# Windowed attention with sinks, then an RWKV channel mix: q kept in even/odd token order and read in steps by the score matmuls

## The chip, the cores and the metric

The kernel runs on one core of one Trainium2 chip. The metric is the device time of one launch in microseconds. All times given for a profile are of one profiled execution; the times of a kernel are those of runs without one.

## What is computed

```python
# q, k, v: (4, 8, 768, 64) = batch, heads, tokens, head size; n_sink = 4, window = 128
scores = (1 / sqrt(64)) * q @ k^T
keep = (key < 4) | ((query - key >= 0) & (query - key < 128))
a = softmax(where(keep, scores, -1e9))
x = (a @ v), heads joined                       # (4, 768, 512)

x_prev = x shifted by one token (zeros first)
xk = mu_k * x + (1 - mu_k) * x_prev             # xr likewise with mu_r
kk = relu(xk @ w_k) ** 2                        # 512 -> 1024
out = sigmoid(xr @ w_r) * (kk @ w_v)            # (4, 768, 512), float32
```

Inputs and output are float32; the kernel multiplies in bf16.

## The kernel before

The work is cut into 12 units of 256 tokens, three per batch entry (u = 3b + T, with T = 0, 1, 2). For each unit there are four stages in the code: `prepare` (casts and transposes of k and q, cast of v), `attend` (scores, exponential, mask, products with v, division), `mix` (transpose of x, the two mixtures xk and xr) and `ffn` (the three products with weights, relu and square, gate, output).

The order in which they run is not the order of the code. Every step is entered in a plan (`P.op`) with an engine, a cost, the data that it reads and writes, and the pool buffers that it takes or holds. The order on each engine is then a fixed list of step numbers (`ORDER`), and for some steps the engine is a fixed choice (`CHOICE`). The planner simulates that order with the costs to decide which buffer of a pool each step gets, and where it puts warm-up matmuls on TensorE (L1019) while TensorE would wait early on. So a step that is left out of the plan would renumber all behind it.

The path of q, which the change touches:

- *Load.* A unit of q is [8 heads, 256 tokens, 64] in float32. For units 0 to 7 (L413) a partition p gets the tokens 2p and 2p + 1 of each head, which lie side by side in memory, so that a row of the transfer has 512 bytes. For units 8 to 11 (`QD`, by `by_dma`) and for units 5 to 11 of k (`KD`) the two halves of 128 tokens are loaded one by one, with rows of 256 bytes (L406).
- *Cast* to bf16 into `qb` (L605, L602), on ScalarE, VectorE or GpSimd.
- *Transpose*, so that the head size lies on the partitions, two heads (a "head pair" c) in 128 partitions. Units 0 to 7: on TensorE through a PSUM bank (L631), one 128 x 128 matmul for the even and one for the odd tokens of each head pair; then a copy (L639) brings the bank to `qt` and, by reading the bank in steps, puts the tokens back into their natural order. Units 8 to 11: by a DMA transpose from `qb` to `qt` (L619), one for each half of 128 tokens, which are in natural order already.
- *Use.* `qt` has the layout [128, head pair, 2, 128]. The sink scores (L697, T > 0) have the keys of the four sinks as stationary operand and all 256 queries of `qt` moving. The window scores (L728) have 64 or 128 keys of one head as stationary operand, in one quarter or half of the array, and 64 to 256 queries moving. Two heads and two halves of the keys run side by side. They are issued two head pairs at a time into two PSUM tiles `sc` (24 matmuls for T > 0, 8 for T = 0). ScalarE then takes the exponential (L787), VectorE multiplies by the mask (L801), and TensorE multiplies by v (L820) and adds the sinks' part (L775).

k takes the same path, and is not changed.

SyncE issues nearly all DMAs, in the order of its list: loads, DMA transposes and outputs (L1015) stand in one queue.

Of the kernel before, what the change touches and what calls it, by code (L numbers as in the profile page):

```python
# [136 lines left out]
    ),  # L137
}

# [1 line left out]
class Plan:  # L141
# [17 lines left out]
    def op(self, engine, cost, emit, rank, reads=(), writes=(), take=(), hold=(), port=False,  # L159
           lag=None, service=0.0, descs=128, mode=0, alts=None, room=2080):  # L160
        i = len(self.ops)
        if i in CHOICE:
            engine = CHOICE[i]
            cost, emit, port = alts[engine]
        self.ops.append(dict(alts=alts,engine=engine, cost=cost, emit=emit, rank=rank, reads=list(reads),
                             writes=list(writes), take=list(take), hold=list(hold), port=port,
                             lag=(1300.0 if service else 90.0) if lag is None else lag,
                             service=service, descs=descs, mode=mode, room=room))

    def schedule(self):  # L170
        ops = self.ops
# [134 lines left out]
def kernel(  # L306
# [14 lines left out]
    nc = tc.nc  # L321
# [67 lines left out]
    def load(u, names, rank, h0=0, h1=H):  # L389
        b, T = divmod(u, NT)  # L390
        for name in names:
            key = (name, u)
            if name == "v":
                for g in range(2):
                    s0 = 256 * T + 128 * g
                    P.op("SP", 600.0, lambda key=key, g=g, s0=s0: nc.sync.dma_start(  # L396
                        out=buf[key][:, g, :, :],
                        in_=v[b, :, s0:s0 + 128, :].rearrange("h p d -> p h d")), rank,
                        service=1250.0, descs=1024, take=[] if g else [("vs", key)],
                        hold=[key] if g else [], writes=[(name, u, g)])  # L400
                continue
            src = {"k": k, "q": q}[name]
            if by_dma(name, u):
                for g in range(2):
                    s0 = 256 * T + 128 * g
                    P.op("SP", 600.0, lambda key=key, src=src, g=g, s0=s0: nc.sync.dma_start(  # L406
                        out=buf[key][:, 4 * g:4 * g + 4, :, :].rearrange("p h j d -> p (h j) d"),
                        in_=src[b, :, s0:s0 + 128, :].rearrange("h p d -> p h d")), rank,
                        service=1250.0, descs=1024, take=[] if g else [(name + "s", key)],
                        hold=[key] if g else [], writes=[(name, u, g)])  # L410
                continue

            P.op("SP", 530.0, lambda key=key, src=src: nc.sync.dma_start(  # L413
                out=buf[key][:, h0:h1, :, :].rearrange("p h j d -> p h (j d)"),
                in_=src[b, h0:h1, 256 * T:256 * T + 256, :].rearrange(
                    "h (p j) d -> p h (j d)", j=2)), rank,
                service=128 * (h1 - h0) * 1.82, descs=128 * (h1 - h0),
                take=[] if h0 else [(name + "s", key)], hold=[key] if h0 else [],
                writes=[(name, u, c) for c in range(h0 // 4, h1 // 4)])

    def load_weight(what, rank):
        name, part = what[:2], what[2:]
# [171 lines left out]
    def prepare(u, rank):  # L594
        b, T = divmod(u, NT)
        for name, half in (("k", 0), ("q", 0), ("k", 1), ("q", 1)):
            key, psk = (name + "t", u), ("prep", u, name, half)
            raw, rk = (name, u), (name + "b", u)
            hs = slice(4 * half, 4 * half + 4)
            def cast(copy, raw=raw, rk=rk, hs=hs, half=half, name=name):  # L600
                if by_dma(name, u):
                    return lambda: copy(  # L602
                        out=buf[rk][:, half, :, :].rearrange("p h d -> p (h d)"),
                        in_=buf[raw][:, hs, :, :].rearrange("p h j d -> p (h j d)"))
                return lambda: copy(  # L605
                    out=buf[rk][:, :, hs, :].rearrange("p j h d -> p h j d"),
                    in_=buf[raw][:, hs, :, :])

            P.op("ACT", act(512), cast(nc.scalar.copy), rank + half,
                 alts={"ACT": (act(512), cast(nc.scalar.copy), False),  # L610
                       "DVE": (dve(512, 0.52), cast(nc.vector.tensor_copy), True),
                       "POOL": (600.0, cast(nc.gpsimd.tensor_copy), True)},
                 take=[] if half else [(name + "b", rk)],
                 hold=[raw] + ([rk] if half else []),
                 reads=[(name, u, half), "table"],
                 writes=[rk + (half,)])

            if by_dma(name, u):
                P.op("SP", 1240.0, lambda key=key, rk=rk, half=half: nc.sync.dma_start_transpose(  # L619
                    out=buf[key][:, :, half, :],  # L620
                    in_=buf[rk][:, half, :, :].rearrange("p h d -> p (h d)")), rank + half,
                    service=930.0, descs=512, lag=1300.0, room=1200, reads=[rk + (half,)],
                    take=[] if half else [(name + "t", key)],
                    hold=[rk] + ([key] if half else []), writes=[key + (half,)])
                continue

            def transpose(half=half, psk=psk, rk=rk):
                ps = buf[psk].bitcast(BF16)[:, 0:512].rearrange("p (j t) -> p j t", j=4)
                for j in range(4):
                    c = 2 * half + j // 2  # L630
                    nc.tensor.transpose(  # L631
                        out=ps[:, j, :], identity=ident,
                        in_=buf[rk][:, j % 2, 2 * c:2 * c + 2, :].rearrange("p a d -> p (a d)"))

            P.op("PE", 225.0, transpose, rank + half, lag=PE_LAG, take=[("bank", psk)],
                 reads=["ident", rk + (half,)], writes=[psk], hold=[rk])

            def evacuate(copy, half=half, psk=psk, key=key):
                return lambda: copy(  # L639
                    out=buf[key][:, 2 * half:2 * half + 2, :, :].rearrange(  # L640
                        "p c g (t j) -> p c (g t) j", j=2),
                    in_=buf[psk].bitcast(BF16)[:, 0:512].rearrange(
                        "p (c j t) -> p c t j", c=2, j=2))

            P.op("ACT", 600.0, evacuate(nc.scalar.copy), rank + half,
                 alts={"ACT": (600.0, evacuate(nc.scalar.copy), False),
                       "DVE": (625.0, evacuate(nc.vector.tensor_copy), False)},
                 hold=[psk] + ([key] if half else []),
                 take=[] if half else [(name + "t", key)],
                 reads=[psk] + ([key + (0,)] if half else []), writes=[key + (half,)])  # L650
# [35 lines left out]
    def attend(u, rank):  # L686
        b, T = divmod(u, NT)
        both = b in JOINT
        if T == 1 or T == 2 and not both:
# [3 lines left out]
            def sink_scores():  # L693
                for i, w in enumerate(us):
                    for c in range(NP):
                        r0 = 32 * (c // 2) + 64 * (c % 2)
                        nc.tensor.matmul(out=buf[psk][r0:r0 + 32, 256 * i:256 * i + 256],  # L697
                                         lhsT=ksink[b % 2][:, 32 * c:32 * c + 32],
                                         rhs=buf["qt", w][:, c, :, :], start=True, stop=True)

            P.op("PE", 150.0 + 109.0 * (len(us) - 1), sink_scores, rank, lag=PE_LAG, mode=2,
                 take=[("bank", psk)], hold=[("qt", w) for w in us], writes=[psk],
# [9 lines left out]
        def scores(k):  # L712
            c = k
            kt, qt, sc = buf["kt", u], buf["qt", u], buf["sc", u, k]
            qs = qt[:, c, :, :].rearrange("p g t -> p (g t)")
            jobs = [(kt[:, c, 0, :], 128, 0, 256), (kt[:, c, 1, :], 384, 128, 256)]
            if T > 0:
                jobs.append((buf["kt", u - 1][:, c, 1, :], 0, 0, 128))
            for (lhs, o0, q0, q1) in jobs:
# [5 lines left out]
                for a in range(2):  # L725
                    rows = slice(64 * a, 64 * a + 64)
                    for keys, f0, f1 in parts:
                        nc.tensor.matmul(out=sc[keys, a, o0 + f0 - q0:o0 + f1 - q0],  # L728
                                         lhsT=lhs[rows, keys], rhs=qs[rows, f0:f1],
                                         start=u not in BIAS, stop=True,  # L730
                                         skip_group_check=u in BIAS)

# [342 lines left out]
```

## Time and profile before

| | |
|---|---|
| time, median of 3 runs | 170.36 us (169.63 to 170.5) |
| span of the profiled execution | 167.0 us (its time with start and end is not listed) |
| TensorE (PE) busy | 159.0 us, 95% of the span |
| VectorE (DVE) busy | 150.6 us, 90% |
| ScalarE (ACT) busy | 127.6 us, 76% |
| GpSimd (POOL) busy | 19.3 us, 12% |
| DMA packets | 80726, of them 61625 under 512 bytes; 33.85 MB |
| mean granted clock of TensorE | 0.990 |

How to read it: the span runs from the first to the last instruction. A row names the line of the kernel, engine, operation, destination and sources, tile of the array or shape, the count, busy time and the mean of one. PEld is TensorE's loading of the stationary operand, which overlaps with its matmuls; SPq is the queue of DMA issues of SyncE. A matmul's duration includes its way through the array, so matmuls overlap; what a group of them occupies is the time from its start to the start of what follows.

### The profile page before, as it was taken

The numbers are of one execution on the slowest core, as the hardware profiler recorded it, in microseconds if no ns is written. First come the engines' busy times: TensorE is split into PE (matmuls) and PEld (weight loads), VectorE is DVE, ScalarE is ACT, GpSimd is POOL, SyncE is SP. The second block draws the span as 40 slices with busy tenths as digits, with TensorE's granted clock in tenths as the row PEclk, the third lists the DMA queues.
The fourth block names the chain that finished last, engine by engine and source line by source line (L and its number), as shares of the span: only waits on it lengthen the run. The fifth ranks groups of instructions, "written<-read, shape, count | busy, mean of one in ns | idle before, by whom it ended". The sixth has DMA issues, their size and how long they took to land.

```text
span 167.0 us, 4741 instructions
## 1 busy us (share of the span) xinstructions
PE 159.0 (95%) x1870; PEld 103.0 (62%) x1870; DVE 150.6 (90%) x391; ACT 127.6 (76%) x210; POOL 19.3 (12%) x46
## 2 busy tenths in 40 slices
PE   7967999999999999999999999999999999999992
PEld 2436566845558666667557675765577575677551
DVE  7179999999999999989999999899999979998941
ACT  3497898998599999988998999889839729652120
POOL 5731020000343121220001000000000000000000
PEclk9996899999999999999999999999999999999999
DMA  4999989999989999889998997896899443410033
GB/s 139 242 291 354 330 219 383 364 216 292 259 219 277 150 266 227 191 206 276 232 182 150 243 265 103 215 211 148 191 203 268 88 92 112 188 67 0 0 135 116
DMA packets 80726, 33.85 MB, mean 203 GB/s; under 512 B 61625, under 2 KB 75201, under 8 KB 80705
## 3 DMA queue, kind: packets, MB, share of 16 engines
q1 hardware_dynamic: 80688, 33.56, 86.3%
q8 instruction: 14, 0.23, 0.6%
q14 instruction: 8, 0.06, 0.1%
q10 hardware_dynamic: 16, 0.00, 0.0%
HBM read 24.12 MB, written 6.29 MB: 182 GB/s over the span
## 4 chain that ended last, share of the span: by engine, by line
PE 78%; ACT 8%; SPq 6%; DMA 5%; issue 1%; DVE 1%
PE bank L950 21%; PE bank L999 21%; PE bank L981 11%; PE bank L820 6%; PE sc L728 5%; DMA ks<-in_k_dram 5%; ACT e L787 3%; PE bank L1019 3%; SPq L396 3%; PE bank L631 3%; PE bank L861 3%; SPq L413 2%; ACT wk_sb L567 2%; PE bank L775 2%; PE bank L697 1%
## 5 line engine op out<-in xcount | busy, mean ns | idle before, releaser
L950 PE MATMUL bank<-xk,wk_sb 128*128 128x256 bf16 x384 | 49.7, 273 | 0.1
L999 PE MATMUL bank<-wv_h,kk 128*128 128x512 bf16 x184 | 46.6, 379 | 0.0
L787 ACT ACTIVATE e<-sc 128x1024 bf16<-128x1024 f32 (+1 forms) x48 | 45.0, 965 | 1.4 <-PE sc L728 1.2
L950 PEld LDWEIGHTS <-wk_sb 128*128 128x128 bf16 x384 | 36.0, 98 | 9.1 <-ACT wk_sb L567 0.5
L960 ACT ACTIVATE rl<-bank 128x512 bf16<-128x512 f32 x40 | 23.4, 605 | 14.8 <-PE bank L950 14.2
L801 DVE TENSOR_TENSOR e<-e,mask 128x1024 bf16<-128x1024 bf16 (+1 forms) x48 | 30.5, 649 | 0.6 <-ACT e L787 0.6
L999 PEld LDWEIGHTS <-kk 128*128 128x128 bf16 x184 | 16.4, 98 | 14.8 <-DVE kk L972 0.5
L981 PE MATMUL bank<-wr_sb,xr 128*128 128x512 bf16 x96 | 24.2, 379 | 0.0
L899 DVE SCALAR_TENSOR_TENSOR xr<-td,mu_all,xt 128x256 bf16<-128x256 bf16 x48 | 23.2, 498 | 0.0
L899 DVE SCALAR_TENSOR_TENSOR xk<-td,mu_all,xt 128x256 bf16<-128x256 bf16 x48 | 21.9, 485 | 0.0
L837 DVE TENSOR_TENSOR x<-bank,rec 128x256 bf16<-128x256 f32 x48 | 19.3, 414 | 0.3
L972 DVE TENSOR_TENSOR kk<-rl 128x512 bf16<-128x512 bf16 x48 | 19.5, 415 | 0.0
L987 ACT ACTIVATE th<-bank 128x512 f32<-128x512 f32 x24 | 14.3, 614 | 5.0 <-PE bank L981 4.8
L820 PE MATMUL bank<-vb,e 128*128 128x65 bf16 x352 | 16.6, 194 | 1.4 <-DVE e L801 0.9
L820 PEld LDWEIGHTS <-e 128*128 128x128 bf16 x352 | 14.3, 98 | 5.5 <-DVE e L801 1.4
L1008 DVE SCALAR_TENSOR_TENSOR ob<-th,bank 128x512 f32<-128x512 f32 x23 | 15.6, 679 | 2.1 <-ACT th L987 1.5
L870 ACT COPY xt<-bank 128x512 bf16<-128x512 bf16 x17 | 10.1, 592 | 5.1 <-PE bank L861 4.6
L981 PEld LDWEIGHTS <-xr 128*128 128x128 bf16 x96 | 8.9, 98 | 7.9
L728 PE MATMUL sc<-qt,kt 64*64 64x128 bf16 (+3 forms) x448 | 12.8, 228 | 0.0
L639 ACT COPY qt<-bank 128x512 bf16<-128x512 bf16 x15 | 9.1, 605 | 3.6 <-PE bank L631 3.6
L728 PEld LDWEIGHTS <-kt 64*64 64x64 bf16 (+1 forms) x448 | 8.9, 108 | 4.5 <-issue 2.8
L1019 PE MATMUL bank<-warm 128*128 128x512 bf16 x33 | 9.5, 429 | 1.1 <-DVE warm L1038 1.1
(71 smaller groups left out, 157.8 us busy)
## 6 DMA issues: line engine op xcount, KB each, us to landing
vs<-in_v_dram SPq DMA_DIRECT2D x24, 256.0 KB, 5.3
out_dram<-ob SPq DMA_DIRECT2D x23, 256.0 KB, 3.3
ks<-in_k_dram SPq DMA_DIRECT2D x16, 256.0 KB, 4.9
qs<-in_q_dram SPq DMA_DIRECT2D x7, 512.0 KB, 5.8
qs<-in_q_dram SPq DMA_DIRECT2D x10, 256.0 KB, 4.5
ks<-in_k_dram SPq DMA_DIRECT2D x4, 512.0 KB, 7.4
w<-in_moe_w_k_dram SPq DMA_DIRECT2D x2, 1024.0 KB, 9.4
w<-in_moe_w_v_dram SPq DMA_DIRECT2D x2, 1024.0 KB, 9.6
```

Of the source, the lines that this page charges most:

```text
L728: nc.tensor.matmul(out=sc[keys, a, o0 + f0 - q0:o0 + f1 - q0], lhsT=lhs[rows, keys], rhs=qs[rows, f0:f1], start=u not in BIAS, stop=True, ...
L787: nc.scalar.activation(out=buf[ek][:, :, lo:], in_=buf[sck][:, :, lo:], func=AF.Exp, scale=scale)
L801: nc.vector.tensor_tensor(out=at, in0=at, in1=m, op=ALU.mult)
L820: nc.tensor.matmul(out=o[:, g, a, :], lhsT=e[:, a, e0:e0 + 128], rhs=rhs, start=(T == 0 and i == 0), stop=(i == len(blocks) - 1), skip_gro ...
L837: P.op("DVE", dve(256), lambda ok=ok, rk=rk, c=c: nc.vector.tensor_tensor(out=buf["x", u][:, :, 128 * c:128 * c + 128].rearrange("p g (a d ...
L899: nc.vector.scalar_tensor_tensor(out=buf[key][:, c, :], in0=buf[tk][:, i, :], scalar=mu[w][:, c:c + 1], in1=xt[:, c, t0 - 1:t0 + 255], op0 ...
L950: nc.tensor.matmul(out=ps[:, i, :], lhsT=wk_sb[:, c, 128 * f:128 * f + 128], rhs=xk[:, c, :], start=(c == 0), stop=(c == NC - 1), skip_gro ...
L960: nc.scalar.activation(out=buf[rk], in_=buf[psk].rearrange("p (i t) -> p i t", i=2), func=AF.Relu)
L972: P.op("DVE", dve(512, 0.52), lambda f2=f2, rk=rk: nc.vector.tensor_tensor(out=buf["kk", u][:, 2 * f2:2 * f2 + 2, :], in0=buf[rk], in1=buf ...
L981: nc.tensor.matmul(out=buf[psk], lhsT=buf["xr", u][:, c, 128 * g:128 * g + 128], rhs=wr_sb[:, c, :], start=(c == 0), stop=(c == NC - 1))
L999: nc.tensor.matmul(out=buf[psk], rhs=wv_h[:, f, :], lhsT=buf["kk", u][:, f, 128 * g:128 * g + 128], start=(f == 0), stop=(f == NF - 1))
L1008: P.op("DVE", dve(512), lambda psk=psk, tk=tk, bk=bk: nc.vector.scalar_tensor_tensor(out=buf[bk], in0=buf[tk], scalar=1.0, in1=buf[psk], o ...
```

## The change

`qt` now keeps the order in which the rows of two tokens give them: for each head pair first the 128 even tokens, then the 128 odd ones. For units 0 to 7 the copy out of the bank takes the elements as they lie. The score and sink matmuls read the queries in natural order all the same, by an access pattern that takes one even token, one odd token, and so on: neighbouring columns are 256 bytes apart in `qt`. For units 8 to 11 q is loaded in one transfer per unit with rows of 512 bytes; the casts take the even tokens of all heads, then the odd ones, out of it, and the DMA transposes put them into the two halves of `qt`. The four second halves of the loads go out of SyncE's list (45, 51, 57, 63), and an empty step (`gap`) keeps the numbers of the others. The costs of the copy L639 in the plan change with it.

```diff
@@ ORDER["SP"]
-        37, 31, 38, 36, 508, 396, 513, 42, 39, 44, 400, 322, 43, 587, 592, 40, 45,
-        480, 667, 50, 41, 669, 48, 671, 673, 49, 51, 46, 47, 563, 56, 559, 54, 745,
-        747, 749, 751, 52, 635, 55, 53, 57, 822, 639, 58, 713, 824, 476, 59, 828, 826,
-        62, 60, 61, 63, 717, 794, 64, 902, 900, 904, 906, 910, 909, 65, 798, 948, 868,
...
+        37, 31, 38, 36, 508, 396, 513, 42, 39, 44, 400, 322, 43, 587, 592, 40, 480,
+        667, 50, 41, 669, 48, 671, 673, 49, 46, 47, 563, 56, 559, 54, 745, 747, 749,
+        751, 52, 635, 55, 53, 822, 639, 58, 713, 824, 476, 59, 828, 826, 62, 60, 61,
+        717, 794, 64, 902, 900, 904, 906, 910, 909, 65, 798, 948, 868, 872, 944, 1016,
...
@@ -166,6 +166,9 @@
                              writes=list(writes), take=list(take), hold=list(hold), port=port,
                              lag=(1300.0 if service else 90.0) if lag is None else lag,
                              service=service, descs=descs, mode=mode, room=room))
+
+    def gap(self):
+        self.ops.append(dict(engine="", reads=[], writes=[], take=[], hold=[]))
 
     def schedule(self):
         ops = self.ops
@@ -400,7 +403,7 @@
                         hold=[key] if g else [], writes=[(name, u, g)])
                 continue
             src = {"k": k, "q": q}[name]
-            if by_dma(name, u):
+            if by_dma(name, u) and name == "k":
                 for g in range(2):
                     s0 = 256 * T + 128 * g
                     P.op("SP", 600.0, lambda key=key, src=src, g=g, s0=s0: nc.sync.dma_start(
@@ -417,6 +420,8 @@
                 service=128 * (h1 - h0) * 1.82, descs=128 * (h1 - h0),
                 take=[] if h0 else [(name + "s", key)], hold=[key] if h0 else [],
                 writes=[(name, u, c) for c in range(h0 // 4, h1 // 4)])
+            if by_dma(name, u):
+                P.gap()
 
     def load_weight(what, rank):
         name, part = what[:2], what[2:]
@@ -598,10 +603,12 @@
             raw, rk = (name, u), (name + "b", u)
             hs = slice(4 * half, 4 * half + 4)
             def cast(copy, raw=raw, rk=rk, hs=hs, half=half, name=name):
-                if by_dma(name, u):
+                if by_dma(name, u) and name == "k":
                     return lambda: copy(
                         out=buf[rk][:, half, :, :].rearrange("p h d -> p (h d)"),
                         in_=buf[raw][:, hs, :, :].rearrange("p h j d -> p (h j d)"))
+                if by_dma(name, u):
+                    return lambda: copy(out=buf[rk][:, half, :, :], in_=buf[raw][:, :, half, :])
                 return lambda: copy(
                     out=buf[rk][:, :, hs, :].rearrange("p j h d -> p h j d"),
                     in_=buf[raw][:, hs, :, :])
@@ -612,7 +619,8 @@
                        "POOL": (600.0, cast(nc.gpsimd.tensor_copy), True)},
                  take=[] if half else [(name + "b", rk)],
                  hold=[raw] + ([rk] if half else []),
-                 reads=[(name, u, half), "table"],
+                 reads=[(name, u, i) for i in
+                       (range(2) if by_dma(name, u) and name == "q" else [half])] + ["table"],
                  writes=[rk + (half,)])
 
             if by_dma(name, u):
@@ -635,16 +643,22 @@
             P.op("PE", 225.0, transpose, rank + half, lag=PE_LAG, take=[("bank", psk)],
                  reads=["ident", rk + (half,)], writes=[psk], hold=[rk])
 
-            def evacuate(copy, half=half, psk=psk, key=key):
+            def evacuate(copy, half=half, psk=psk, key=key, name=name):
+                if name == "q":
+                    return lambda: copy(
+                        out=buf[key][:, 2 * half:2 * half + 2, :, :].rearrange(
+                            "p c j t -> p (c j t)"),
+                        in_=buf[psk].bitcast(BF16)[:, 0:512])
                 return lambda: copy(
                     out=buf[key][:, 2 * half:2 * half + 2, :, :].rearrange(
                         "p c g (t j) -> p c (g t) j", j=2),
                     in_=buf[psk].bitcast(BF16)[:, 0:512].rearrange(
                         "p (c j t) -> p c t j", c=2, j=2))
 
-            P.op("ACT", 600.0, evacuate(nc.scalar.copy), rank + half,
-                 alts={"ACT": (600.0, evacuate(nc.scalar.copy), False),
-                       "DVE": (625.0, evacuate(nc.vector.tensor_copy), False)},
+            ns = (act(512), dve(512, 0.54)) if name == "q" else (600.0, 625.0)
+            P.op("ACT", ns[0], evacuate(nc.scalar.copy), rank + half,
+                 alts={"ACT": (ns[0], evacuate(nc.scalar.copy), False),
+                       "DVE": (ns[1], evacuate(nc.vector.tensor_copy), name == "q")},
                  hold=[psk] + ([key] if half else []),
                  take=[] if half else [(name + "t", key)],
                  reads=[psk] + ([key + (0,)] if half else []), writes=[key + (half,)])
@@ -696,7 +710,8 @@
                         r0 = 32 * (c // 2) + 64 * (c % 2)
                         nc.tensor.matmul(out=buf[psk][r0:r0 + 32, 256 * i:256 * i + 256],
                                          lhsT=ksink[b % 2][:, 32 * c:32 * c + 32],
-                                         rhs=buf["qt", w][:, c, :, :], start=True, stop=True)
+                                         rhs=buf["qt", w][:, c, :, :].rearrange("p j t -> p t j"),
+                                         start=True, stop=True)
 
             P.op("PE", 150.0 + 109.0 * (len(us) - 1), sink_scores, rank, lag=PE_LAG, mode=2,
                  take=[("bank", psk)], hold=[("qt", w) for w in us], writes=[psk],
@@ -712,7 +727,7 @@
         def scores(k):
             c = k
             kt, qt, sc = buf["kt", u], buf["qt", u], buf["sc", u, k]
-            qs = qt[:, c, :, :].rearrange("p g t -> p (g t)")
+            qs = qt[:, c, :, :].rearrange("p j t -> p t j")
             jobs = [(kt[:, c, 0, :], 128, 0, 256), (kt[:, c, 1, :], 384, 128, 256)]
             if T > 0:
                 jobs.append((buf["kt", u - 1][:, c, 1, :], 0, 0, 128))
@@ -726,7 +741,7 @@
                     rows = slice(64 * a, 64 * a + 64)
                     for keys, f0, f1 in parts:
                         nc.tensor.matmul(out=sc[keys, a, o0 + f0 - q0:o0 + f1 - q0],
-                                         lhsT=lhs[rows, keys], rhs=qs[rows, f0:f1],
+                                         lhsT=lhs[rows, keys], rhs=qs[rows, f0 // 2:f1 // 2, :],
                                          start=u not in BIAS, stop=True,
                                          skip_group_check=u in BIAS)
 
```

2 rows, old and new, of the table ORDER are left out of this document.

## The prediction

> **What bounds the kernel now.** I read the page's busy shares first, then the stretches, then PE's waits, then the PE timeline around the score matmuls, and last the groups by shape and SyncE's queue.
>
> ```profile
> PE 159.0 (95%) x1870; PEld 103.0 (62%) x1870; DVE 150.6 (90%) x391; ACT 127.6 (76%) x210; POOL 19.3 (12%) x46
> 16.00:26.00 10.00, 9.51 (x139) 6.25 (x138) 9.81 (x23) 9.58 (x14) 0.86 (x1) 0.92 0.99 294
> 26.00:36.00 10.00, 9.77 (x111) 6.59 (x107) 9.96 (x27) 9.30 (x17) 0.00 (x0) 1.00 1.00 313
> 36.00:44.00 8.00, 7.97 (x110) 4.39 (x108) 7.99 (x22) 6.22 (x11) 0.52 (x1) 1.00 1.13 293
> 44.00:60.00 16.00, 15.79 (x200) 10.76 (x199) 15.68 (x41) 15.10 (x27) 4.73 (x9) 1.00 1.12 218
> 60.00:80.00 20.00, 20.00 (x285) 14.21 (x284) 19.07 (x48) 18.64 (x32) 3.97 (x6) 1.00 1.03 231
> 100.00:120.00 20.00, 20.00 (x212) 12.39 (x211) 19.38 (x52) 18.06 (x31) 0.38 (x2) 1.00 0.82 174
> ```
>
> The first line is the share of each engine, the others are stretches (start:end, length, then PE, PEld, DVE, ACT, POOL busy, granted clock, DMA share, GB/s). Busy alone would not show that PE streams at its limit, but the chain that ended last does: from 44 us on it is nearly all PE, and a gate or value product of four 512-column matmuls takes 0.86 us in it, that is 216 ns each, again and again. The granted clock there is 1.00. So from 44 us to the last product (161.8 us) the end is set by PE's work alone. PE's idle time from 16 to 60 us is 0.49 + 0.23 + 0.03 + 0.21 = 0.96 us, and nothing to speak of later. From 25.7 to 43.4 us the chain runs through SyncE and a load of k, but PE is 98% busy beside it, so both are near the bound there.
>
> The score matmuls are what the change touches on PE. The PE timeline (start, length until the last one ends, tile and count):
>
> ```profile
> 66.86 0.29 PE L697 MATMUL bank<-qt,ksink 128*32 128x256 bf16 x4
> 67.08 0.53 PE L728 MATMUL sc<-qt,kt 64*64 64x192 bf16 x24
> 67.55 0.40 PE L631 MATMUL bank<-ident,qb 128*128 128x128 bf16 x4
> ...
> 45.27 0.50 PE L728 MATMUL sc<-qt,kt 64*128 64x256 bf16 x8
> 45.71 1.04 PE L999 MATMUL bank<-wv_h,kk 128*128 128x512 bf16 x4
> ```
>
> Start to next start is what a group occupies: 0.47 us for a pair of head pairs with a window to the left (24 matmuls), 0.44 us without one (8 matmuls), 0.22 us for the four sink matmuls. Sixteen more matmuls cost only 0.03 us, so instructions don't set this. Columns do: in both cases each tile of the array streams 2 x 384 = 768 query columns, with the tiles side by side. The price of a column follows from the groups by shape, (379 - 273)/256 = 0.41 ns and (273 - 193)/192 = 0.42 ns from 512, 256 and 64 columns; 768 columns are 0.32 us, and 0.12 to 0.15 us per group is entry and drain. The sink group fits: 256 columns are 0.107 us and 0.11 us goes beside it.
>
> **The change on PE.** It moves no instruction. Compared in program order, each engine issues the same list, but for one warm-up matmul fewer (two gone before 11 us, one added later), four SyncE issues fewer, and other PSUM banks. The number of query columns is the same, so a score matmul can't become shorter. What changes is how a column is found: until now 64 to 256 neighbouring bf16 of `qt` went through, now the reader alternates between the even and the odd half, 256 bytes apart, at every column. No matmul of the trace reads like that, so I bound it.
>
> ```profile
> L870 ACT COPY xt<-bank 128x512 bf16<-128x512 bf16 x17 | 10.1, 592 | 5.1 <-PE bank L861 4.6 <-DVE e L801 0.4
> L639 ACT COPY qt<-bank 128x512 bf16<-128x512 bf16 x15 | 9.1, 605 | 3.6 <-PE bank L631 3.6
> L870 DVE COPY xt<-bank 128x512 bf16<-128x512 bf16 x5 | 2.1, 416 | 0.2
> L639 DVE COPY qt<-bank 128x512 bf16<-128x512 bf16 x1 | 0.7, 691 | 0.1
> ```
>
> These are groups by shape (count, busy us, mean ns): the same 512 elements read in a run (L870) and read alternating 256 bytes apart (L639), out of PSUM. For ScalarE it costs 13 ns, 0.025 ns an element. ScalarE needs (1041 - 605)/512 = 0.85 ns an element anyway (exponentials of 1024, relu of 512), half TensorE's pace. For VectorE, which is faster than that as long as neighbours lie together, it costs 691 - 416 = 275 ns, 0.54 ns an element. So the low end is 0.025 and the high end 0.54 ns a column. TensorE at 0.42 ns is the fast reader, so the row nearest to it is VectorE's: I take that the advantage of neighbours is lost and TensorE falls to one column in 0.83 ns, ScalarE's pace, 0.417 ns more per column.
>
> [...]
>
> The sum: 12 units of work x 2 groups x 768 columns x 0.417 ns = 24 x 0.320 = 7.7 us; 8 sink groups x 256 x 0.417 = 8 x 0.107 = 0.86 us; together 8.5 us (bounds: 0.5 us at 0.025 ns, 11.1 us at 0.54 ns). Of that, 6 score and 2 sink groups (2.1 us) run before 44 us, where PE has idle time to give and the chain is partly SyncE's. I count 1.0 us as hidden, the idle time of 16 to 60 us (bounds 0 and 2.1). The other 18 score and 6 sink groups add 6.4 us to a saturated engine, with no cover. On the path: 8.5 - 1.0 = +7.5 us.
>
> **The other parts.**
> - Emptying transposed q: on ScalarE 15 copies x 13 ns = 0.2 us less, on VectorE one copy 0.27 us less. Both wait for PE at other places (ScalarE 14 us at L960), so 0; if they were on the path, -0.5 us.
> - Casts of the loaded q of units 8 to 11: runs of 64 floats, as L605 has them (630 ns against 627 ns for L602 on ScalarE): 0.
> - Loads: eight of 256 KB become four of 512 KB, placed where the first halves stood; both casts of a unit now wait for the whole.
>
> ```profile
> qs<-in_q_dram SPq DMA_DIRECT2D x7, 512.0 KB, 5.8
> qs<-in_q_dram SPq DMA_DIRECT2D x10, 256.0 KB, 4.5
> ...
> 120.19 0.58 SPq L406 DMA_DIRECT2D qs<-in_q_dram  x1
> ...
> 122.23 0.90 SPq L406 DMA_DIRECT2D qs<-in_q_dram  x1
> ...
> 127.42 1.58 SPq L619 DMA_TRANSPOSE qt<-qb  x1
> ```
>
> So a first cast may come 5.8 - 4.5 = 1.3 us later, a second one earlier. Unit 11 has the least room: issued at 120.2 us, landed by 126.0, cast at 126.98, transposed from 127.4 to 132.0 + 3.5 us of landing, read by the scores at 137.7 us: 2 us of cover on PE, so 0. Without that cover it is at most 1.3 us for each of four units, and VectorE, ScalarE or SyncE would stand behind the waiting cast. The four second issues that go took 0.37, 0.57, 2.24 and 0.90 us (at 79.4, 90.3, 106.0 and 122.2 us), 4.1 us of SyncE's time; v, outputs and transposes behind them start earlier. PE has no wait after 60 us that this could shorten: 0.
>
> The time: span 167.0 + 7.5 = 174.5 us. The listing gives the profiled execution no time but its span; the median of the three runs, 170.36, lies 3.4 us above that (start and end). So 170.36 + 7.5 = **177.9 us**.
>
> **The rivals.**
> 1. *Alternating reads are free on PE* (ScalarE's row holds). Then everything that is left lies beside a saturated PE: 170.36, less the 0.2 us of one warm-up matmul, plus up to 0.5 us: 169.9 to 170.9, no change. For it: ScalarE's 13 ns; the value-of-sink product L676 reads in runs of 64 and takes 384 ns for 512 columns, against 379 for L999 in one run. Against it: VectorE's row, and that no reader of the trace keeps 0.42 ns an element over such a pattern.
> 2. *Free reads, and the lighter SyncE queue makes it faster.* The place is the feed of k, v and q behind the four issues; it would have to give PE more than 0.85 us, and PE's only idle time after 16 us is 0.96 us, nearly all ahead of the first shortened load (71.7 us). At best the 0.2 us of warm-up and 0.47 us of copies at places that release the early chain: 169.7; it passes 0.5% only if all of this and half of the idle time go: 169.2.
> [...]
> 4. *More than half rate*: at VectorE's 0.54 ns 11.1 - 1.0: 180.5. Speaks for it that up to four streams read at once; against it that ScalarE copes with 0.85 ns.
>
> **How the numbers follow.** Half rate, 176.5 to 179.2 by what is hidden (2.1 to 0 us, and 0.3 us of scatter): 0.54. Rival 3: 0.09, rival 4: 0.06. Rival 1: 0.24, rival 2: 0.07. Within 0.5% (0.85 us, about what a measurement of this kernel tells from no change) falls 0.20 of the free cases; faster by more, rival 2 and a little of rival 1: 0.08; slower by more gets the rest, 0.72: half rate, rivals 3 and 4 (0.69) and 0.03 for a free read with a late cast. Range: down to the free case, 169.8, and up to 180.0, short of rival 4's middle. The slower cases by themselves: 173 to 180.5.
>
> **What would show it.** Right: the score groups take 0.79 and 0.76 us from start to next start instead of 0.47 and 0.44, the sinks 0.33 instead of 0.22; 64x192 takes 258 + 80 = 338 ns, 64x64 193 + 27 = 220 ns; other groups unchanged; PE's busy share as high over a longer span. The loads appear as eleven of 512 KB and two of 256 KB, packets under 512 B fall by 8192, `qt` copies take about 592 ns on ScalarE and 416 on VectorE. Wrong: score matmuls with the old durations (rival 1); or a longer span with those durations and new PE waits on `qt` or `qb`, which would put the loss on the loads.

## The result and the profile after

The changed kernel takes 177.12 us in the median (176.93 to 177.61, 4 runs) against 170.0 us (169.31 to 170.5, 4 runs): 1.0444 times the time of before, 95% interval 1.0413 to 1.0475 (the two medians alone give 1.042). The profiled execution, which is one of the four, took 176.93 us with a span of 174.9 us; the span of before was 167.0 us. In all runs that list both, time and span lie 2.0 to 2.2 us apart, so the profiled execution of before took about 169.1 us, an estimate, and was faster than its median: the spans differ by 7.9 us, the medians by 7.1 us.

Three lines of the page of the kernel after and a stretch of it, with the columns as in those of before:

```profile
PE 167.9 (96%) x1869; PEld 106.0 (61%) x1869; DVE 151.6 (87%) x391; ACT 128.9 (74%) x210; POOL 19.8 (11%) x46
DMA packets 76565, 33.85 MB, mean 194 GB/s; under 512 B 53368, under 2 KB 71040, under 8 KB 76544
PE 89%; DVE 6%; ACT 2%; issue 1%; DVEq 0%
60.00:80.00 20.00, 20.00 (x252) 13.17 (x249) 18.41 (x43) 17.21 (x31) 4.15 (x6) 1.00 1.05 232
```

PE is busy 8.9 us longer with one matmul fewer, the granted clock in the stretch shown is still 1.00, and the chain that ended last is now 89% PE (the third line), against 78% on the page of before:

```profile
PE 78%; ACT 8%; SPq 6%; DMA 5%; issue 1%; DVE 1%
```

The PE timeline of after shows which matmuls grew (start, length to the last end, tile, count):

```profile
69.19 0.43 PE L711 MATMUL bank<-qt,ksink 128*32 128x256 bf16 x4
69.54 0.92 PE L743 MATMUL sc<-qt,kt 64*64 64x192 bf16 x24
70.40 0.40 PE L639 MATMUL bank<-ident,qb 128*128 128x128 bf16 x4
...
45.57 0.90 PE L743 MATMUL sc<-qt,kt 64*128 64x256 bf16 x8
46.40 1.04 PE L1014 MATMUL bank<-wv_h,kk 128*128 128x512 bf16 x4
```

From start to next start a score group now takes 0.86 us (24 matmuls) and 0.83 us (8), where it took 0.47 and 0.44; the sinks take 0.35 us in place of 0.22. The groups by shape (busy us, mean ns) say the same per column, and show that what does not read `qt` is unchanged (L965, 273 ns, as L950 before). The first three lines are of before, the others of after:

```profile
L728 PE MATMUL sc<-qt,kt 64*64 64x192 bf16 x128 | 7.3, 258 | 0.0
L728 PE MATMUL sc<-qt,kt 64*64 64x64 bf16 x128 | 7.0, 193 | 0.0
L728 PE MATMUL sc<-qt,kt 64*128 64x256 bf16 x32 | 3.6, 274 | 0.0
L743 PE MATMUL sc<-qt,kt 64*64 64x192 bf16 x128 | 11.5, 350 | 0.0
L743 PE MATMUL sc<-qt,kt 64*64 64x64 bf16 x128 | 11.1, 221 | 0.0
L743 PE MATMUL sc<-qt,kt 64*128 64x256 bf16 x32 | 6.2, 405 | 0.1
L965 PE MATMUL bank<-xk,wk_sb 128*128 128x256 bf16 x384 | 49.3, 273 | 0.0
L648 ACT COPY qt<-bank 128x512 bf16<-128x512 bf16 x15 | 8.8, 589 | 4.7 <-PE bank L639 4.7
L648 DVE COPY qt<-bank 128x512 bf16<-128x512 bf16 x1 | 0.4, 425 | 0.1
```

256 columns went from 274 to 405 ns: (405 - 274)/256 = 0.51 ns more per column. The groups say the same, 0.39 us for 768 columns and 0.13 us for the sinks' 256, whether two tiles of the array stream side by side (the group of 8), or four (the group of 24 and the sinks). The slope between 256 and 64 columns is (405 - 221)/192 = 0.96 ns a column, where it was 0.42.

### The profile page after: what moved, and what is told of

Its sections match the earlier page's. It is cut to its first block, busy times and chain, and to the rows that moved or that the text cites. A ratio compares the mean times of both kernels' runs of the same rounds, so it can differ in the third digit from the quotient of the medians.

```text
span 174.9 us, 4737 instructions
## 1 busy us (share of the span) xinstructions
PE 167.9 (96%) x1869; PEld 106.0 (61%) x1869; DVE 151.6 (87%) x391; ACT 128.9 (74%) x210; POOL 19.8 (11%) x46
## 4 chain that ended last, share of the span: by engine, by line
PE 89%; DVE 6%; ACT 2%; issue 1%; DVEq 0%
PE bank L1014 23%; PE bank L965 23%; PE bank L996 12%; PE sc L743 11%; PE bank L835 6%; PE bank L876 3%; PE bank L639 3%; PE bank L1034 3%; DVE e L816 2%; PE bank L790 2%; PE bank L711 2%; ACT e L802 1%; PE bank L935 1%; DVE rl L979 1%; DVE x L852 1%
## 5 line engine op out<-in xcount | busy, mean ns | idle before, releaser
L965 PE MATMUL bank<-xk,wk_sb 128*128 128x256 bf16 x384 | 49.3, 273 | 0.0
L965 PEld LDWEIGHTS <-wk_sb 128*128 128x128 bf16 x384 | 36.1, 98 | 9.1 <-issue 1.0
L816 DVE TENSOR_TENSOR e<-e,mask 128x1024 bf16<-128x1024 bf16 (+1 forms) x48 | 31.3, 665 | 0.7 <-ACT e L802 0.6
L914 DVE SCALAR_TENSOR_TENSOR xk<-td,mu_all,xt 128x256 bf16<-128x256 bf16 x48 | 22.6, 502 | 0.0
L914 DVE SCALAR_TENSOR_TENSOR xr<-td,mu_all,xt 128x256 bf16<-128x256 bf16 x48 | 22.3, 480 | 0.0
L743 PE MATMUL sc<-qt,kt 64*64 64x128 bf16 (+2 forms) x448 | 21.9, 292 | 0.1
L987 DVE TENSOR_TENSOR kk<-rl 128x512 bf16<-128x512 bf16 x48 | 20.0, 425 | 0.0
L743 PEld LDWEIGHTS <-kt 64*64 64x64 bf16 (+1 forms) x448 | 11.9, 106 | 8.7 <-issue 3.1
L849 DVE RECIPROCAL rec<-bank 128x4 f32<-128x4 f32 x48 | 8.1, 177 | 6.7 <-PE bank L835 5.9
```

The source lines that it names most:

```text
L816: nc.vector.tensor_tensor(out=at, in0=at, in1=m, op=ALU.mult)
L914: nc.vector.scalar_tensor_tensor(out=buf[key][:, c, :], in0=buf[tk][:, i, :], scalar=mu[w][:, c:c + 1], in1=xt[:, c, t0 - 1:t0 + 255], op0 ...
L965: nc.tensor.matmul(out=ps[:, i, :], lhsT=wk_sb[:, c, 128 * f:128 * f + 128], rhs=xk[:, c, :], start=(c == 0), stop=(c == NC - 1), skip_gro ...
L987: P.op("DVE", dve(512, 0.52), lambda f2=f2, rk=rk: nc.vector.tensor_tensor(out=buf["kk", u][:, 2 * f2:2 * f2 + 2, :], in0=buf[rk], in1=buf ...
```

## The experiments

**What belongs to the read, and what to the rest?** The first run undoes the alternating read alone, everything else stays changed:

```diff
-            qs = qt[:, c, :, :].rearrange("p j t -> p t j")
+            qs = qt[:, c, :, :].rearrange("p j t -> p (j t)")
-                                         lhsT=lhs[rows, keys], rhs=qs[rows, f0 // 2:f1 // 2, :],
+                                         lhsT=lhs[rows, keys], rhs=qs[rows, f0:f1],
# and the sink matmuls: rhs=buf["qt", w][:, c, :, :]
```

> The changed kernel with one thing undone: score and sink matmuls read qt in a run of neighbouring columns, as it lies. The queries then come out in even/odd order, so the output is that of permuted queries; loads, casts, copies, order and the number of columns are those of the changed kernel. Theory READ (the alternating read on TensorE is the whole loss): the time of the kernel before, 170.0 us within 0.5 us, score groups back at 0.47 and 0.44 us. Rival LOADS (a part of the loss is from the single 512 KB loads and the casts that wait for them): 171 to 174 us with score groups of 0.47 us.

Measured: 169.44 us (12 runs) beside 169.67 us of the kernel before, ratio 0.9979, interval 0.9954 to 1.0005, with the old durations (and 0.46 us for a group of 24, 0.43 us for a group of 8):

```profile
L743 PE MATMUL sc<-qt,kt 64*64 64x192 bf16 x128 | 7.3, 258 | 0.0
L743 PE MATMUL sc<-qt,kt 64*128 64x256 bf16 x32 | 3.6, 273 | 0.1
```

So, within that interval, the read is the whole loss; the time is 0.56 us below the 170.0 us of the expectation, but 0.23 us below what the kernel before took beside it. The single loads, the casts that wait for them, the four SyncE issues and the cheaper copies together move the time by less than this measurement tells; LOADS falls.

**Can the steps go to the write?** Here the result stays in natural order, but `qt` is read in two runs and PSUM is written in steps of two columns:

```diff
-                        nc.tensor.matmul(out=sc[keys, a, o0 + f0 - q0:o0 + f1 - q0],
-                                         lhsT=lhs[rows, keys], rhs=qs[rows, f0 // 2:f1 // 2, :],
+                        nc.tensor.matmul(out=sc[keys, a, o0 + f0 - q0:o0 + f1 - q0].rearrange(
+                                             "p (t j) -> p j t", j=2),
+                                         lhsT=lhs[rows, keys], rhs=qt[rows, c, :, f0 // 2:f1 // 2],
# and the sink matmuls in the same way
```

> The changed kernel, with the steps moved to the other side: the matmuls read qt in two runs, first even then odd tokens, and write their columns in steps of two into PSUM, so the scores stand in natural order and the result is the reference's. READ with a write that takes steps freely: 170.0 us within 0.5 us. READ with a write that is as dear as the read (0.5 ns a column): 177 us again. If steps cost more on the write side, over 178 us.

Measured: 175.84 us (5 runs), ratio 1.035 (1.0325 to 1.0374) to the kernel before; score matmuls of 192 columns at 348 ns, of 256 at 401 ns.

```profile
L744 PE MATMUL sc<-qt,kt 64*128 64x256 bf16 x32 | 5.7, 401 | 0.1
69.46 0.85 PE L744 MATMUL sc<-qt,kt 64*64 64x192 bf16 x24
```

The single matmuls take as long as with the alternating read, but the groups are less dear: what follows this one starts at 70.24 us, 0.78 us after it, 0.31 us more than before, where the read adds 0.39 us. By time the write costs 6.4 us over the first run, against 7.7 us for the read (177.12 us, measured in another series). So it is about four fifths as dear, between the first two expectations and near the second. TensorE doesn't take this reordering for nothing on either side.

**Where is the loss hidden?** Two runs keep the alternating read in the first three units alone, and in the others alone:

```diff
-                                         lhsT=lhs[rows, keys], rhs=qs[rows, f0 // 2:f1 // 2, :],
+                                         lhsT=lhs[rows, keys], rhs=(qs[rows, f0 // 2:f1 // 2, :] if u < 3 else
+                                              qt[:, c, :, :].rearrange("p j t -> p (j t)")[rows, f0:f1]),
# the sink matmuls likewise; the other run has u >= 3
```

> The changed kernel with the alternating read in units 0 to 2 alone (6 of 24 score groups, 2 of 8 sink groups); the later units read in a run, so their queries come out in even/odd order. In the two profiles the same score group starts at 45.3 us before and 45.6 us after, so theory HIDDEN (before 44 us TensorE waits for data, not for itself): 0.3 us over e1_run. If the first units are on the path in full: 6 x 0.385 + 2 x 0.13 = 2.6 us over e1_run; by the prediction's count (1.0 us hidden): 1.6 us over it.

> The changed kernel with the alternating read in units 3 to 11 alone (18 score groups, 6 sink groups); units 0 to 2 read in a run, so their queries come out in even/odd order. HIDDEN: 18 x 0.385 + 6 x 0.13 = 7.7 us over e1_run, nearly the whole loss. If the first units are on the path too: as much as the whole loss less 2.6 us, about 4.8 us over e1_run.

Measured: 170.11 us (12 runs) with the first units and 176.21 us (6 runs) with the others, on the chip of the first run, e1_run in the expectations (169.44 us). The first three units cost 0.7 us of the 2.6 us that their groups grow by, the other nine 6.8 us. Each of these differences is good to some 0.7 us, an estimate from the intervals of the ratios: 1.0019 (0.9989 to 1.0049) and 1.0376 (1.0354 to 1.0399), against 0.9979 (0.9954 to 1.0005). The 1.6 and 2.6 us for the first units and the 4.8 us for the others fall; HIDDEN comes nearest (0.3 and 7.7 us), but the other units cost 0.9 us less than it says. Together the two make 7.4 of the 7.7 us between 177.12 and 169.44 us.

**What makes a read dear?** The prediction argued that neighbouring columns must lie together, from VectorE's copies (416 ns in a run, 691 ns alternating); PAIR puts that as two columns in 4 bytes. Four runs give the kernel before other patterns of the same number of columns; the first reads two tokens, then two 256 bytes on:

```diff
-            qs = qt[:, c, :, :].rearrange("p g t -> p (g t)")
+            qs = qt[:, c, :, :].rearrange("p g (t r) -> p t g r", r=2)
-                                         lhsT=lhs[rows, keys], rhs=qs[rows, f0:f1],
+                                         lhsT=lhs[rows, keys], rhs=qs[rows, f0 // 4:f1 // 4, :, :],
# the sink matmuls likewise
```

> The kernel before (qt in natural order), with score and sink matmuls that read two neighbouring tokens (4 bytes), then two of the other half 256 bytes on, and so on; the queries come out in another order, and loads, copies and columns are those of the kernel before. Theory PAIR (TensorE keeps its pace only where two columns lie together in 4 bytes): free, score matmuls of 192 columns at 258 ns, time 169.7 us. [...] Rival LOOP (each jump of the access pattern costs, here one per 2 columns instead of one per column): half of the loss, 192 columns at about 305 ns, 173.5 us.

The second has `r=8` and `f0 // 16:f1 // 16`, eight neighbouring columns before each jump of 256 bytes, by PAIR as free as two:

> As the run with two neighbouring tokens, but eight (16 bytes) at a time before the jump of 256 bytes; the queries come out in another order. [...] LOOP: an eighth of the loss, 192 columns at about 270 ns, 170.6 us.

The third and fourth step through the 512 queries of two head pairs, by 2 and by 8 elements, that is 4 and 16 bytes (the fourth with `r=8` and `4 * (c % 2) + f0 // 64:4 * (c % 2) + f1 // 64, :`, in runs of 64 columns). Their products are those of other queries than the reference's; the number of columns is the same:

```diff
+            qs = qt.rearrange("p c g t -> p (c g t)")[:, 512 * (c // 2):512 * (c // 2) + 512].rearrange(
+                "p (m r) -> p r m", r=2)
+                                         lhsT=lhs[rows, keys], rhs=qs[rows, c % 2, f0:f1],
```

> [...] PAIR: the whole loss, 192 columns at 350 ns, 177 us. [...] LOOP: free.

> [...] PAIR: the whole loss, 350 ns, 177 us. [...] LOOP: free, 258 ns, 169.7 us.

The score matmuls of 192 columns in the groups by shape, one line from each run in that order:

```profile
L728 PE MATMUL sc<-qt,kt 64*64 64x192 bf16 x128 | 7.9, 269 | 0.0
```
```profile
L728 PE MATMUL sc<-qt,kt 64*64 64x192 bf16 x128 | 7.3, 258 | 0.0
```
```profile
L729 PE MATMUL sc<-qt,kt 64*64 64x192 bf16 x128 | 7.2, 254 | 0.0
```
```profile
L729 PE MATMUL sc<-qt,kt 64*64 64x192 bf16 x128 | 16.7, 511 | 0.0
```

Times against the kernel before: 1.0064 (1.0032 to 1.0096), 0.9983 (0.9945 to 1.0022), 1.0018 (0.9986 to 1.005) and 1.1377 (1.1321 to 1.1434). The product with w_k (L950 or L951, 256 columns), which does not read `qt`, stays at 273 ns in all of them. PAIR falls: steps of 4 bytes cost nothing that could be told, though no two columns lie together. LOOP falls: two columns per jump cost 11 of the 92 ns for 192 columns, an eighth and not half, and steps of 16 bytes cost a lot, though their jump back comes only once in 64 columns. Two columns per jump are not quite free (0.64% of the time), and neither theory has the size of the last run: PAIR put 177 us and LOOP 169.7 us, where it took 193.49 us.

So steps of 16 bytes, which come back beside an element only after 64 columns, cost more (511 ns for 192 columns) than the changed read, which comes back after two (350 ns), unless it is the distance that counts. Two more runs, each one execution with a profile, separate the distance (DISTANCE) from the return (RETURN). The first alternates at every column between two places 16 bytes apart, eight times each, and then goes on to the next 32 bytes; the second makes three steps of 256 bytes, then goes back to 16 bytes behind the first of the four places, and so comes back beside an element only after 64 columns; its products are those of other queries. If the return is what counts, 192 columns should take about 350 ns in the first, as in the changed kernel, and 511 ns in the second, as with steps of 16 bytes:

```diff
+            qs = qt[:, c, :, :].rearrange("p g (m s r) -> p (g m) r s", s=2, r=8)
+                                         lhsT=lhs[rows, keys], rhs=qs[rows, f0 // 16:f1 // 16, :, :],
# the second: 512 queries as "p (a b r) -> p r b a", a=4, r=8; b = steps of 16 bytes, a = steps of 256 bytes
```

> [...] Theory DISTANCE (what matters is how far a jump goes, and 16 bytes is the dear one): 192 columns at 511 ns as in the run with steps of 16 bytes. [...]

> [...] DISTANCE: 350 ns for 192 columns, as the jumps of 256 bytes in the changed kernel. [...]

```profile
L728 PE MATMUL sc<-qt,kt 64*64 64x192 bf16 x128 | 11.5, 349 | 0.0
```
```profile
L729 PE MATMUL sc<-qt,kt 64*64 64x192 bf16 x128 | 16.9, 515 | 0.0
```

RETURN holds, and DISTANCE falls: 349 ns with a step of 16 bytes there and back, 515 ns with steps of 256 bytes that come back beside an element only after 64 columns. The first of the two also adds an alternating read alone, as dear as that of the change, to the kernel before: 177.91 us beside 170.48 us, 7.4 us more by one execution of each.

## Why the prediction was right

- *TensorE sets the end from 44 us on.* Right. The first score group of unit 3 starts at 45.27 us in the profile before and at 45.57 us after; from there to the start of the last product (161.77 and 169.72 us) it is 116.5 and 124.15 us, 7.65 us more. By the groups as measured it should be 18 x 0.39 + 6 x 0.13 = 7.8 us, so in these profiles next to nothing covered it. The same stretch takes 116.38 us in the profile of the first run and 124.17 us in that of the run with units 3 to 11, again 7.8 us. The medians of these two runs are only 6.8 us apart; the profiled execution of the first was the fastest of its twelve, and where the other 1.0 us lies stays open.
- *Price of a column.* The sign and the order were right, the size too small and the reason wrong. I put 0.417 ns (ScalarE's pace); it is 0.51 ns, near VectorE's 0.54, which I had as the upper bound. A group grew by 0.39 us, not 0.32, and the sum of all is 24 x 0.39 + 8 x 0.13 = 10.4 us, not 8.5. The reason given, that neighbouring columns must lie together, is refuted by the steps of 4 bytes (254 ns for 192 columns). ScalarE's row, which spoke for a free read, could not tell: it reads PSUM, it is at 0.85 ns an element, and the trace had no other reader at 0.42 ns. With the reason refuted, it was luck that ScalarE's pace came near the measured one. No run shows the alternating read at a part of the price, which the chances count at 0.09 (rival 3): it cost 0.51 ns a column in the changed kernel and (406 - 274)/256 = 0.52 ns between places 16 bytes apart.
- *The part that is hidden.* Put at 1.0 us, by PE's idle time. In the two profiles 2.3 us of the first units' 2.6 us are gone by unit 3. One pair of profiles tells little here: in the five in which the first units lose nothing (before, the first run, units 3 to 11 alone, runs of eight, steps of 4 bytes) that score group starts anywhere from 44.77 to 46.19 us. By medians the run with the read in units 0 to 2 alone loses 0.7 us, so about 1.9 us are hidden. Busy time misled: before 44 us the chain of before ran through ScalarE, SyncE and a load of k (from 35.55 to 43.34 us), and PE's "98% busy" held waits that do not show as idle time. The same four products with w_r take 1.07 us from start to next start before (first two lines) and 0.87 us after (last two lines), yet only 0.03 us of it shows as idle time, since the last one ends 1.04 us after the start of the first in both:

```profile
36.76 1.04 PE L981 MATMUL bank<-wr_sb,xr 128*128 128x512 bf16 x4
37.83 1.04 PE L999 MATMUL bank<-wv_h,kk 128*128 128x512 bf16 x4
37.48 1.04 PE L996 MATMUL bank<-wr_sb,xr 128*128 128x512 bf16 x4
38.35 1.03 PE L1014 MATMUL bank<-wv_h,kk 128*128 128x512 bf16 x4
```

- *How the two sizes add up.* The growth was put 1.9 us too small and the hidden part 0.9 to 1.3 us too small. These errors pull the time in opposite directions, so it is partly luck that 177.9 us came so close to 177.12 us. With both as measured the sum is 10.4 less 1.9 to 2.3, that is 8.1 to 8.5 us; the spans differ by 7.9 us, the ratio makes it 7.5 us and the medians 7.1 us. The rest is not explained. The 3.4 us that I called start and end is also wrong: it is 2.0 to 2.2 us, and the rest is that the profiled execution was a fast one. The sum did not use it.
- *Everything else at nothing.* Right: 0.9979 (0.9954 to 1.0005) for all of it. The copies came to 589 and 425 ns, the packets under 512 bytes fell by 8257 (8192 forecast), and PE has no new wait on `qt` or `qb`. So a free read (rival 1) would have meant no change, as put there; rival 2, a gain from the lighter queue, found nothing to shorten.
- *What the price depends on.* By the runs, two columns per jump cost 0.64% of the time, eight per jump and steps of 4 bytes nothing that could be told (0.9983 and 1.0018), one per jump 4.4%. Alternating between two places costs 0.51 ns a column more, steps of 16 bytes (617 - 274)/256 = 1.34 ns more. The changed read comes back to each half at every second column, and is less than half as dear as these steps.

## What to carry to other kernels

Where TensorE is the bound, leave reorderings to an engine with time to spare: ScalarE's copy out of PSUM put the tokens in order for 13 of its 605 ns, the same reordering in the matmul's operand cost 131 ns on top of 274. Before stepping through a moving operand, look at how far the steps go and how soon the read comes back: here steps of 4 bytes and jumps after eight columns cost nothing that could be told, jumps after two 0.64% of the time, after every column 4.4%, and steps of 16 bytes 13.8%. To judge what longer work on an engine costs in an early phase, follow the chain that ended last and compare starts with starts, not the busy share.

## What the runs showed of the hardware

- The moving operand of TensorE, read in steps of 4 bytes, costs nothing that could be told: 254 ns for 192 columns and 278 for 256, against 258 and 274 for neighbouring columns. Jumps of 256 bytes after every 8 columns leave it at 258 and 274 ns. With a jump after every 2 columns 256 columns take 299 ns, after every column 405 ns.
- Alternating costs the same whether the two places are 16 or 256 bytes apart (349 and 350 ns for 192 columns). Where the read comes back beside an element only after 64 columns, a column takes (617 - 292)/192 = 1.7 ns by 256 and 64 columns, with steps of 16 as with steps of 256 bytes (511 and 515 ns for 192). Why an early return is cheaper was not tried further.
- Writing to every second float32 of PSUM takes 401 ns for 256 columns, nearly as long as the alternating read; a group of 24 such matmuls takes 0.78 us, against 0.86 us.

The 1.7 ns above come from these two lines of the run with steps of 16 bytes:

```profile
L729 PE MATMUL sc<-qt,kt 64*128 64x256 bf16 x32 | 9.9, 617 | 0.0
L729 PE MATMUL sc<-qt,kt 64*64 64x64 bf16 x128 | 17.0, 292 | 0.0
```
